# Expert jobs of a fused state-space, MLP and mixture-of-experts kernel: second products three jobs behind, in 256 columns

## The chip, the cores and the metric

The kernel runs on one core of a Trainium2 chip. The metric is the device time of one execution in microseconds (us), as the median of several runs. Profiles come from one further execution each.

## The reference

Three stages, all on 3072 tokens of 256 values. The first is a state-space recurrence over chunks of 32 positions, the second an MLP, the third a mixture of 8 experts of which each token takes one.

```python
# 1: state space, batch 4, 8 heads, 768 positions, head width 32, state 16
M = (Cc @ Bc.T) * L                       # within a chunk, causal decay L
y = M @ xc + (Cc @ state) * exp(cum)      # and from the state before the chunk
state = decay_full * state + sum(Bx)
# 2: MLP, 256 -> 2048 -> 256
x = maximum(x @ w_in, 0) ** 2 @ w_out
# 3: one expert of 8 for each token, 256 -> 1024 -> 256
idx = argmax(xn @ en.T / tau)             # xn, en: rows divided by their norms
gate = softmax(xn @ en.T / tau)[idx]
out[t] = gate[t] * (maximum(x[t] @ w1[idx], 0) @ w2[idx])
```

## The kernel before

The tokens are 24 tiles of 128, in 6 groups of 4 tiles. Every matrix that enters a product is split into two f16 parts, a high and a low one, and a product is the sum of three: high with high, high with low, low with high.

The order of all instructions is written out when the kernel is built, by `weave`. Each piece of work is a generator ("thread") that yields steps: an engine letter (T TensorE, S ScalarE, V VectorE, G GpSimd, Q SyncE's DMA queue), a cost, and the instructions of the step. `weave` keeps a clock for each engine and takes the thread that can start first; among those within a small slack of it, the one with the smallest due time. Due times and some choices of engine are the constants in `DUE`. The order so made is each engine's program: an engine executes its instructions strictly in that order and waits at each for what it needs. `need` and `order` hold a thread back until another has yielded a `mark`.

First come the state-space tiles and, woven with them, the MLP. Its first group runs as f32 products (`unit0`, `unit0_out`), the five others as units (`unit`): a first product of 6 matmuls of 512 columns (L1001), relu and square, a split, and a second product of 12 matmuls of 256 columns (L1037). ScalarE or VectorE squares, by the shares s0 to s2 of `DUE`. Meanwhile the experts' weights are loaded, scaled and split into `W` (`expert`).

When a group of tokens has passed the MLP, `finish` evicts each tile, scales and splits it into a row of f16 halves, turns the row by a DMA transpose on SyncE's queue (`turn`, L387) and makes the logits (L1086). `route` picks each token's expert and its place, and scatters the rows into `xs` in HBM, sorted by expert (L1186). The last 4 values of a row, its "end", hold a factor and the token's number.

A job is a block of 128 rows of one expert. Jobs 0 to 12 (`J1` = 13) are blocks already full from the first five groups. The last group completes the table (`other_jobs`), eight pad blocks are written behind the rows (`pads`, L1518), and the rest follow: 28 jobs always, up to 31 if needed. `job_load` brings a block in, turned, by a DMA transpose (L1333), and its ends by a second, small DMA (L1336), both on SyncE's queue. `job` then has

- a first product into two banks of 512 columns, 12 matmuls (L1363); `job_relu` evicts each bank by ScalarE (high part) and VectorE (low part) into one of 2 buffers `rh`;
- a turn of `rh` into one of 3 buffers `rT` by a DMA transpose on SyncE's queue (L1374);
- a second product of 8 pairs, into a bank of 512 columns: the high part of the rows with both halves of the weights side by side (512 columns, L1390), then the low part with the high half (256 columns, L1392);
- the output: VectorE multiplies the row's factor by the job's (L1398), ScalarE scales columns 256 to 511 (L1400), VectorE scales columns 0 to 255 and adds (L1403), and GpSimd scatters the rows to `out` (L1406).

The expert's number sits in a register of TensorE, so each product's weights have an address that is worked out by a register instruction. The second product of job j is held back until the first product of job j + 2 stands in the order:

```python
yield "order", ("m1j", min(j + 2, JU - 1))
yield "need", ("out", j - 2)
```

At the very start idle TensorE is kept going by dummy products (`keep_warm`, L373).

## Time and profile before

| | |
|---|---|
| median of 3 runs | 530.54 us (529.8 to 534.5) |
| profiled execution | 528.94 us |
| its span, first to last instruction | 527.2 us |
| mean granted TensorE clock | 0.986 of full speed |
| busy: TensorE, VectorE, ScalarE, GpSimd | 95%, 58%, 65%, 30% of the span |
| first product of the first job begins | 358.29 us |
| last instruction of GpSimd ends | 521.1 us |

Times within the execution count from its first instruction. [...] In brackets behind an instruction stands how long its engine was idle before it, and what ended that wait.

### The profile page before, as it was taken

How to read it: one execution, taken by the hardware profiler on the slowest of the kernel's cores; microseconds unless marked ns; L12 is line 12 of the kernel's file. 1: busy time of each engine (PE TensorE's matmuls, PEld its weight loads, DVE VectorE, ACT ScalarE, POOL GpSimd, SP SyncE). 2: the span in 40 equal slices, each digit the busy share in tenths (PEclk: the TensorE clock that was granted, in tenths of full speed). 3: DMA queues.
4: the chain of work that ended last, by engine and by line, in shares of the span. 5: the costliest groups of instructions: out<-in, count | busy, mean ns of one | idle time of the engine just before them, and what ended most of it. 6: DMA issues, size and time to landing. Idle time of an engine off the chain costs nothing. (4 is left out here: it accounts for less than half of the span.)

```text
span 527.2 us, 11441 instructions
## 1 busy us (share of the span) xinstructions
PE 499.4 (95%) x3888; PEld 315.3 (60%) x3888; DVE 308.1 (58%) x856; ACT 342.7 (65%) x725; POOL 159.1 (30%) x189
## 2 busy tenths in 40 slices
PE   7799999999999999999999999999979999998992
PEld 6564456887666676667666766674535555554551
DVE  3668978517988878676457548837345343432330
ACT  6578868119879989999999999865222333322320
POOL 1454657301564337301410320500113311120212
PEclk9999999999999999999999999999979999998998
DMA  8970132424182631293313322025799977887651
GB/s 291 411 272 2 29 92 62 114 108 130 30 205 81 141 101 54 90 203 99 130 72 79 153 90 42 32 52 99 124 143 176 217 158 143 147 134 146 131 118 38
DMA packets 114377, 65.07 MB, mean 123 GB/s; under 512 B 103429, under 2 KB 107791, under 8 KB 111248
## 3 DMA queue, kind: packets, MB, share of 16 engines
q1 hardware_dynamic: 111824, 57.93, 44.9%
q0 software_dynamic: 2496, 6.40, 4.0%
q8 instruction: 34, 0.56, 0.4%
q14 instruction: 23, 0.19, 0.1%
HBM read 32.58 MB, written 8.13 MB: 77 GB/s over the span
## 5 line engine op out<-in xcount | busy, mean ns | idle before, releaser
L1037 PE MATMUL bank<-work 128*128 128x256 f16 x960 | 115.6, 273 | 1.2 <-issue 0.8
L1001 PE MATMUL bank<-work 128*128 128x512 f16 x480 | 114.4, 379 | 0.7 <-ACT work L1006 0.7
L1037 PEld LDWEIGHTS <-work 128*128 128x128 f16 x960 | 92.2, 98 | 20.7 <-issue 1.8
L1390 PE MATMUL bank<-wexp,work 128*128 x224 | 77.7, 392 | 6.7 <-DMA work<-work 6.1
L1363 PE MATMUL bank<-wexp,work 128*128 x336 | 77.6, 381 | 0.4 <-DMA work<-xs 0.4
L1001 PEld LDWEIGHTS <-work 128*128 128x128 f16 x480 | 45.8, 99 | 45.1 <-issue 2.1
L1406 POOL DMA_INDIRECT out<-work x28 | 27.6, 985 | 130.0 <-DVE work L1403 111.3
L1416 ACT ACTIVATE work<-bank 128x512 f16<-128x512 f32 x56 | 32.8, 597 | 46.2 <-PE bank L1363 25.0
L1392 PE MATMUL bank<-wexp,work 128*128 x224 | 62.8, 280 | 0.0
L1418 DVE SCALAR_TENSOR_TENSOR work<-bank,work 128x512 f16<-128x512 f32 x56 | 38.2, 689 | 42.1 <-ACT work L1416 41.8
L1025 POOL TENSOR_TENSOR work<-work 128x512 f16<-128x512 f32 x20 | 24.3, 1217 | 104.5 <-ACT work L1018 90.6
L1363 PEld LDWEIGHTS <-work 128*128 128x128 f16 x336 | 32.9, 99 | 37.8 <-issue 1.4
L706 POOL TENSOR_SCALAR_AFFINE_SELECT wexp<-wexp 128x512 f32<-128x512 f32 x48 | 39.2, 816 | 51.5 <-DVE wexp L698 33.4
L1022 DVE TENSOR_TENSOR work<-work 128x512 f16<-128x512 f32 x60 | 42.6, 713 | 20.0 <-ACT work L1018 18.9
L1006 ACT ACTIVATE work<-bank 128x512 f32<-128x512 f32 x80 | 46.7, 591 | 9.6 <-PE bank L1001 9.3
L1400 ACT ACTIVATE work<-bank,work 128x256 f32<-128x256 f32 x28 | 13.3, 474 | 59.0 <-PE bank L1392 57.1
L1018 ACT CAST work<-work 128x512 f16<-128x512 f32 x80 | 48.8, 613 | 0.8 <-DVE work L1014 0.4
L698 DVE TENSOR_TENSOR wexp<-bank,wexp 128x256 f32<-128x256 f32 x96 | 38.1, 416 | 15.1 <-PE bank L690 9.1
L1390 PEld LDWEIGHTS <-work 128*128 128x128 f16 x224 | 22.4, 100 | 35.4 <-DMA work<-work 7.1
L1403 DVE SCALAR_TENSOR_TENSOR work<-bank,work 128x256 f32<-128x256 f32 x28 | 13.5, 484 | 49.2 <-ACT work L1400 47.2
L1011 ACT ACTIVATE work<-work 128x512 f32<-128x512 f32 x64 | 39.9, 629 | 0.6
L1186 POOL DMA_INDIRECT xs<-work x24 | 28.5, 1190 | 35.9 <-DVE work L1182 14.6
(211 smaller groups left out, 747.9 us busy)
## 6 DMA issues: line engine op xcount, KB each, us to landing
wexp<-in_w SPq DMA_DIRECT2D x8, 1024.0 KB
work<-in_w SPq DMA_DIRECT2D x8, 1024.0 KB
wexp<-in_w_in SPq DMA_DIRECT2D x4, 1024.0 KB
wexp<-in_w_out SPq DMA_DIRECT2D x4, 1024.0 KB
wexp<-in_x SPq DMA_DIRECT2D x6, 512.0 KB
wexp<-in_ct SPq DMA_DIRECT2D x6, 256.0 KB
wexp<-in_bc SPq DMA_DIRECT2D x6, 256.0 KB
xs<-work SPq DMA_DIRECT2D x9, 132.0 KB
```

The source lines that it names most:

```text
L698: V.tensor_tensor(mv, ps.rearrange("p (a b) -> p a b", b=32), eg[:, t, n * q:n * q + n].rearrange("p h q -> p (h q)").unsqueeze(2) .to_bro ...
L706: G.affine_select(out=mm, in_=mm, pattern=[[0, 4], [1, P]], compare_op=ALU.is_ge, fill=0.0, base=0, channel_multiplier=-1)
L1001: T.matmul(p, win[:, wi, kk, f * P:(f + 1) * P], x[:, xi * 2 + kk], start=(n == 0), stop=(n == 5))
L1006: S.activation(r, p, AF.Relu, scale=XK)
L1011: S.activation(r, r, AF.Square)
L1018: S.copy(gh, r)
L1022: V.tensor_tensor(gl, r, gh, ALU.subtract)
L1037: T.matmul(po, gg[:, s], wout[:, wi, f], start=(f == 0 and n == 0 and k % 2 == 0), stop=(f == NF - 1 and n == 2), skip_group_check=True)
L1363: T.matmul(p, xj[i][:, xi * 2 + kk], W[:, bass.ds(e, 1), c0:c0 + 512].rearrange("p a b -> p (a b)"), start=(n == 0), stop=(n == 5))
L1390: T.matmul(po, r[:, f], W[:, bass.ds(e, 1), c0:c0 + 512].rearrange("p a b -> p (a b)"), start=(f == 0), stop=False, skip_group_check=True)
L1392: T.matmul(po[:, 0:DM], r[:, 8 + f], W[:, bass.ds(e, 1), c0:c0 + 256].rearrange("p a b -> p (a b)"), start=False, stop=(f == 7), skip_grou ...
L1418: V.scalar_tensor_tensor(out=rh[:, 1, s], in0=p, scalar=0.0, in1=rh[:, 0, s], op0=ALU.max, op1=ALU.subtract)
```

## The change

1. The second product of job j is held back until the first product of job j + 3; there are 4 buffers `rT` instead of 3, and job j's turn of `rh` waits for the second product of j - 4.
2. The second product runs into 256 columns: 8 times three matmuls of 256 columns, the three parts into the same place. So the output is one ScalarE step that scales by the factor; L1400's buffer and VectorE's addition (L1403) are gone.
3. The ends of a job's rows are loaded by a new thread `job_ends`, issued by ScalarE's queue, after the turn of `rh`; behind it stands VectorE's multiplication of the factors. ScalarE gets registers with the row numbers (`ends_rows`).
4. In the last group `finish` turns the rows by 4 TensorE transposes a tile into bank 3 (f16) and one VectorE copy, instead of the DMA transpose.
5. `pads` waits for the last rows of the first table (`xj`) and no longer for their ends (`fi`).
6. Costs in the threads that `weave` counts with, and all of `DUE`, are others, so the whole order is another.

```diff
-           d0=6.529, m0=251.382, m1=-31.115, u1=21.067, du=31.584, t0=-3.93, t1=-0.257, t2=51.405, t3=-77.002,
...
-           fj=73.378, fe=93.207, oj=-46.052, pd=-14.956, oe=40.303, lj=0, l0=-53.773, v0=0.5, v1=0.75, v2=0.75,
...
+           g0=-87.702, g1=1, g2=0, g3=-57.34, dl=0, dl1=0, s0=558470754, s1=0.25, s2=0.25, bs=2, qx=24.864, qb=8.052,
...
+           emb=83.454, con=43.583, fj=93.688, fe=40.743, oj=85.543, pd=28.762, oe=-59.404, lj=51.301, l0=85.543,
...
+    ident_h = A.take([P], F16)
...
-                free["R"] = s + 3.4
-                th[2] = s + 4.0
+                free["R"] = s + 2.4
+                free["D"] = max(free["D"], s) + 0.5
+                th[2] = s + 3.6
...
-        yield "T", 1.296, (u % 2,)
+        yield "T", 1.307, (u % 2,)
...
-        yield from turn(xo, row[:, 0:2 * DM], 0.45)
+        if g < NGRP - 1:
+            yield from turn(xo, row[:, 0:2 * DM], 0.45)
+        else:
+            for i in (2, 3):
+                yield "need", ("ev", 4 * g + i)
+            yield "order", ("xo", k - 1)
+            pt = bank[3].bitcast(F16)[:, 512 * (k % 2):512 * (k % 2) + 512].rearrange("p (c a) -> p c a", a=P)
+            yield "T", 0.3, (3,)
+            for c in range(4):
+                T.transpose(pt[:, c], row[:, c * P:c * P + P], ident_h)
+            yield "V", 0.35, (3,)
+            V.tensor_copy(xo, pt)
+            yield "mark", ("xo", k)
...
-    rT = [OW.take([16, P], F16) for _ in range(3)]
+    rT = [OW.take([16, P], F16) for _ in range(4)]
     res = [OW.take([DM], F32) for _ in range(6)]
-    tbb = [OW.take([DM], F32) for _ in range(2)]
...
-        yield "Q", 1.27, 0.45
+        yield "Q", 1.33, 0.8, -0.35
         reads_rows(Q.dma_start_transpose(out=xj[i].bitcast(I16), in_=row_at(r, 0, 512)), table)
         yield "mark", ("xj", j)
-        yield "Q", 0.48, 0.06
-        reads_rows(Q.dma_start(fi[i].bitcast(I16), row_at(r, 512, 516)), table)
-        yield "mark", ("fi", j)
...
-        yield "need", ("m2j", j - 3)
-        if j < 3:
+        yield "need", ("m2j", j - 4)
+        if j < 4:
             yield "need", ("m2", NF * NGRP - 1)
-        yield "Q", 2.2, 1.8, 0.8
-        Q.dma_start_transpose(out=rT[j % 3], in_=flat(rh))
+        yield "Q", 2.4, 2.6, -0.5
+        Q.dma_start_transpose(out=rT[j % 4], in_=flat(rh))
         yield "mark", ("rT", j)
+        yield "spawn", job_ends(j, table)
         yield "due", job_due(j)
 
-        yield "order", ("m1j", min(j + 2, JU - 1))
+        yield "order", ("m1j", min(j + 3, JU - 1) if j < JU else j)
...
-        yield "T", 2.6, (pb[j % 2],)
+        r = rT[j % 4]
+        po = bank[pb[j % 2]][:, 0:DM]
+        yield "T", 2.64, (pb[j % 2],)
         for f in range(8):
-            c0 = 4096 + f * 512
-            T.matmul(po, r[:, f], W[:, bass.ds(e, 1), c0:c0 + 512].rearrange("p a b -> p (a b)"), start=(f == 0),
-                     stop=False, skip_group_check=True)
-            T.matmul(po[:, 0:DM], r[:, 8 + f], W[:, bass.ds(e, 1), c0:c0 + 256].rearrange("p a b -> p (a b)"),
-                     start=False, stop=(f == 7), skip_group_check=True)
+            for ri, wi in ((0, 0), (0, 1), (1, 0)):
+                c0 = 4096 + f * 512 + wi * DM
+                T.matmul(po, r[:, 8 * ri + f], W[:, bass.ds(e, 1), c0:c0 + DM].rearrange("p a b -> p (a b)"),
+                         start=(f == 0 and ri + wi == 0), stop=(f == 7 and ri == 1), skip_group_check=True)
...
-        yield "V", 0.1, "L"
-        V.tensor_tensor(ff, fi[i][:, 0:2].bitcast(F32), fjob[:, j:j + 1], ALU.mult)
-        yield "S", 0.47, (pb[j % 2],)
-        S.activation(tbb[j % 2], po[:, DM:2 * DM], AF.Copy, scale=ff)
         yield "need", ("sent", j - 6)
-        yield "V", 0.4, (pb[j % 2],)
-        V.scalar_tensor_tensor(out=res[j % 6], in0=po[:, 0:DM], scalar=ff, in1=tbb[j % 2], op0=ALU.mult, op1=ALU.add)
+        yield "S", 0.36, (pb[j % 2],)
+        S.activation(res[j % 6], po, AF.Copy, scale=ff)
...
+    def job_ends(j, table):
+        i = j % NXJ
+        yield "need", ("rows_s", table)
+        yield "need", ("out", j - 2)
+        yield "need", ("sent", j - NXJ)
+        yield "S", 0.45
+        reads_rows(S.dma_start(fi[i].bitcast(I16), xs[bass.ds(rows_s[j], P), 512:516]), table)
+        yield "V", 0.1, "L"
+        V.tensor_tensor(ffj[j % 2], fi[i][:, 0:2].bitcast(F32), fjob[:, j:j + 1], ALU.mult)
+        yield "mark", ("fi", j)
...
+    def ends_rows(table, ap, n):
+        yield "need", ("tab", table)
+        if table:
+            yield "need", ("jr1", J1 - 3)
+        yield "S", 1.0
+        rows_s.extend(load_regs(ap[0:1, 0:n], n, ACT, DUMMY))
+        yield "mark", ("rows_s", table)
...
-        yield "need", ("fi", J1 - 1)
+        yield "need", ("xj", J1 - 1)
         for e in range(E):
-            yield "Q", 0.86, 0.4
+            yield "Q", 0.6, 0.3
```

## Rows read from the trace of the kernel before

**Rows 1.** Stretches of the whole span: busy time by engine, granted clock, DMA share.

```profile
core 0: us, PE busy (x) PEld busy (x) DVE busy (x) ACT busy (x) POOL busy (x), PEclk, DMA share, GB/s
...
0.00:40.00 40.00, 32.37 (x396) 24.00 (x396) 21.88 (x72) 26.56 (x53) 16.11 (x34) 1.00 0.85 321
...
40.00:358.29 318.29, 314.72 (x2675) 212.20 (x2676) 221.79 (x607) 266.21 (x572) 111.40 (x124) 1.00 0.33 91
...
377.00:396.00 19.00, 14.10 (x89) 7.22 (x87) 8.40 (x36) 4.33 (x9) 2.95 (x3) 0.83 0.85 134
...
250.00:300.00 50.00, 48.93 (x370) 33.70 (x369) 29.31 (x76) 49.66 (x102) 13.28 (x11) 1.00 0.32 114
```

**Rows 2.** Who TensorE waited for, whole span: total us, times, longest.

```profile
PE bank L1390 <- DMA work<-work: 6.1, 3, 2.9
...
PE bank L1086 <- DMA work<-work: 1.3, 3, 0.8
...
PE bank L663 <- DVE work L916: 0.8, 1, 0.8
...
PE bank L1390 <- SPq L1594: 0.6, 1, 0.6
```

**Rows 3.** TensorE in order of time, 378 to 398 us; idle before in brackets.

```profile
378.98 0.38 PE L1390 MATMUL bank<-wexp,work 128*128 x1 [1.08 <-DMA work<-work]
...
390.98 0.59 PE L1390 MATMUL bank<-wexp,work 128*128 x1 [2.94 <-DMA work<-work]
...
397.56 0.38 PE L1390 MATMUL bank<-wexp,work 128*128 x1
```

**Rows 4.** TensorE in order of time, 430 to 484 us.

```profile
430.67 2.75 PE L1363 MATMUL bank<-wexp,work 128*128 x12 [0.41 <-DMA work<-xs]
...
446.24 2.75 PE L1363 MATMUL bank<-wexp,work 128*128 x12
...
448.83 0.38 PE L1390 MATMUL bank<-wexp,work 128*128 x1
...
451.43 1.89 PE L1363 MATMUL bank<-wexp,work 128*128 x8
...
477.01 0.38 PE L1390 MATMUL bank<-wexp,work 128*128 x1 [2.07 <-DMA work<-work]
...
483.91 0.38 PE L1390 MATMUL bank<-wexp,work 128*128 x1
```

**Rows 5.** SyncE's queue in order of time: DMA instructions, start and duration.

```profile
377.80 2.57 SPq L387 DMA_TRANSPOSE work<-work  x2
...
421.71 0.34 SPq L1518 DMA_DIRECT2D xs<-work  x1
...
426.31 2.79 SPq L1333 DMA_TRANSPOSE work<-xs  x2
...
471.36 3.18 SPq L1374 DMA_TRANSPOSE work<-work  x1
```

**Rows 6.** TensorE in order of time, the MLP's last units.

```profile
346.88 1.47 PE L1037 MATMUL bank<-work 128*128 128x256 f16 x12
...
348.19 2.75 PE L1001 MATMUL bank<-work 128*128 128x512 f16 x12
```

**Rows 7.** L1363 (357 to 360 us), L1390 (378.8 to 381): durations, starts.

```profile
L1363 PEldq FUSED_REGOPS  x21: 51/55/65, 357.1 to 359.9; - x21
...
L1363 PE MATMUL bank<-wexp,work x8: 379/379/379, 358.3 to 359.8; 128*128 x8
...
L1390 PEldq FUSED_REGOPS  x8: 55/55/55, 378.9 to 380.8; - x8
```

**Rows 8.** TensorE's groups by line and shape, 40 to 358.2 us.

```profile
L793 PE MATMUL bank<-wexp 128*128 128x128 f32 x40 | 7.8, 278 | 0.0
```

**Rows 9.** Line L1336, whole span: loads of row ends.

```profile
L1336 SPq DMA_DIRECT2D work<-xs x28: 333/430/1082, 351.3 to 479.3; - x28
```

**Rows 10.** VectorE in order of time, the end.

```profile
519.21 0.48 DVE L1403 SCALAR_TENSOR_TENSOR work<-bank,work 128x256 f32<-128x256 f32 x1 [2.84 <-ACT work L1400]
```

## The prediction

> **What bounds the kernel now.** Read the stretches first [rows 1]. Up to 358.29 us TensorE loses 7.63 us of the first 40 (the start, which is also padded with dummy products) and 3.57 us of the next 318: that part is bound by TensorE's own work. The expert jobs follow. [...] Read next who TensorE waited for [rows 2]: the largest entry is L1390, the second product of a job, three times, for the DMA that turns its rows (rT). Last read those places in order of time [rows 3, 4]. In an undisturbed job the first product takes 448.83 - 446.24 = 2.59 us and the second 451.43 - 448.83 = 2.60 us, 5.19 us together [rows 4], and there TensorE is never idle. So a job is bound by columns streamed, and what can be won is the disturbed places, the start, and the tail.

> **What it removes.** Times in us, from the profiled execution.
> The waits of L1390 for rT: 1.08 at 378.98, 2.94 at 390.98 [rows 3], 2.07 at 477.01 [rows 4]; 6.09. Why rT is late: SyncE's queue is served in order. Two of the last group's four row turns (L387) stand in it at 377.80 for 2.57, just where the rT turns are needed, and in the other place one rT turn, issued at 471.36, held the queue for 3.18 by itself [rows 5] and landed some 5.6 after its issue. Three jobs of distance with a fourth rT buffer put one more first and one more second product, 5.2, between a job's first product and its second. Each of the three waits is shorter than that.
> The slower clock behind two of them: from 390.98 to 397.56 a second product and half a first took 6.58 where 2.60 + 1.30 is due, 2.68 lost [rows 3]; from 477.01 to 483.91 a whole pair took 6.90 for 5.19, 1.71 lost [rows 4]. Sum 4.39; with no wait of 2 to 3 us ahead of it the clock has no occasion to fall.
> The logits' wait for the turned rows (L1086), 0.8 at its longest [rows 2]: TensorE now turns them itself. I leave its other two waits standing.
> The wait for job 13's rows, 0.41 [rows 4], and that of the last job for its rT, 0.6 [rows 2], which gets one more product of cover.
> The tail: after the last second product ScalarE scales one half and VectorE adds the other (0.48 [rows 10]); VectorE's step goes. 0.48. On the earlier 27 jobs that step lay beside TensorE's work and its removal is worth nothing.
> Sum removed: 6.09 + 4.39 + 0.8 + 0.41 + 0.6 + 0.48 = 12.77.

> **What it adds.**
> Columns: the second product was 8 x (512 + 256) columns in 16 instructions and is 24 x 256 in 24. The MLP's second product has that very form: 12 of 128x256 take 348.19 - 346.88 = 1.31 [rows 6], so 24 take 2.62 against 2.60. 28 x 0.02 = 0.56.
> Issue: unlike the MLP's, a job's products take their weights' address from a register, and each carries one register instruction on TensorE's sequencer. How fast can that go? Where the sequencer starts ahead of the array it issued 21 of them from 357.1 to 359.9, 2.8 / 20 = 0.14 each; after the wait at 378.9 eight at L1390, with as many of L1392 between, took 1.9, that is 1.9 / 14 = 0.136 each [rows 7]. The array needs 0.109 for 256 columns and 0.216 for 512. So a second product that starts with nothing issued ahead takes 24 x 0.136 = 3.26, 0.64 too long, while a first product gives the sequencer time: 12 x (0.216 - 0.136) = 0.96. Alternating, a job needs 36 x 0.136 = 4.9 of sequencer in 5.21 of array: hidden, with a cover of 0.3. By 359.9 the sequencer was some 13 products ahead of the array (21 issued, 8 begun) [rows 7], and a second product eats about 5 of them. The cover is gone where second products follow each other: the order now ends with four in a row (jobs 24 to 27), and three of them have no first product ahead. 3 x 0.64 less the 0.3 still in hand = 1.6. Bounds: 0 (if the queue holds more) and, where it fails everywhere, a rival below.
> Turning the last group's rows: 16 products of 128 columns. No row has them in f16; half of the 0.109 for 256 columns is 0.055 [rows 6], the f32 turns of L793 cost 7.8 / 40 = 0.195 [rows 8]. Between 0.88 and 3.1 in all; I take 0.88, since a 16-bit product of that width is the nearer form. TensorE pays it in full, as it is the bound. VectorE's four copies of 128x512 (an estimate: at most twice the 0.48 of a 128x256 step [rows 10]) lie beside it.
> [...]
> Row ends on ScalarE's queue: an issue costs 0.43, at most 1.08 [rows 9]. It leaves SyncE, where it stood ahead of rT turns, and lands on ScalarE, which in the jobs is busy for about a quarter of the time (4.33 of 19 [rows 1]): worth nothing either way by itself. But VectorE's multiplication by the ends' factor now stands right behind the issue in VectorE's order, so VectorE waits for the landing, and behind it waits the next job's second relu step. That step has time: the bank it frees is wanted two jobs later, 2 x 5.19 less the first product's 2.59 and the relu steps themselves. Up to some 6 us of landing (an estimate from [rows 4]) it costs nothing.
> Residual: a new order of this length will have some wait of its own; I take one of the removed size, 1.08 + 0.41 = 1.5 (bounds 0 and 4).
> Sum added: 0.56 + 1.6 + 0.88 + 1.5 = 4.54.

> **The first 358 us.** All due times change, so the order of everything does. What it can give back is part of 7.63 + 3.57 idle [rows 1]; it can as well add as much. For it: the embeddings' preparation is put far later, and TensorE waited 0.8 for its VectorE steps [rows 2]; and most squares of groups 2 to 5 move from ScalarE, busy for 49.66 of 50 us where TensorE lost 1.07, to VectorE, busy for 29.31 [rows 1]. I take a gain of 1.0, bounds 5 either way.

> **The sum.** -12.77 + 4.54 - 1.0 = -9.2. The profiled execution took 528.94 (span 527.2 and 1.7 around it), which is 1.6 below the median of the runs, 530.54. So 519.7 by the profiled execution, and 521.3 for the median.

> **Rivals.**
> The gain turns into a wait for job 13's rows. Its row turns were issued at 426.31, after eight pad writes of which the last stood at 421.71 [rows 5], each between rT turns; TensorE already waited for them [rows 4]. If this chain keeps its place in time, all that is saved ahead of 430 is waited for there, and only 2.07 + 1.71 + 0.6 + 0.48 less 0.3 and 1.6 is left: about -3, 527.5. Against it: the chain starts with the last group's logits, which no longer queue for SyncE behind rT turns.
> The new order of the first 358 us loses 5 where I take a gain of 1: 527.3.
> Slower: TensorE's sequencer binds in every job, because it reaches each second product with nothing issued ahead (it stands at a semaphore for rT or for a bank until the array has caught up). Then the 0.64 comes 28 times, 18 us, and the sum is -12.77 + 0.56 + 0.88 + 1.5 - 1.0 + 18 = +7.2: 537.7. It decides when the lead over the array at the start of a second product is below some 5 products. Against it: the 13 products of lead [rows 7].
> A change that doesn't do what it says, with rT still late because the transfers themselves are slow, would keep the 6.09 and the clock's 4.39 in part; the residual's upper bound and the first rival cover it.

> **How the numbers follow.** The forecast has 0.69, job 13's rows 0.13, the lost start 0.10, the starved array 0.08. The forecast's own span, from no residual, no burst and 5 gained at the start to the bounds on the other side (turns at 0.195, residual 4), is 514 to 526. The range takes in the two middling rivals and ends at 529; only the starved array is outside, with a little on the fast side. About 1% is what a measurement here can tell from no change, 525.2 to 535.8: faster 0.72, most of the forecast and the lucky end of the first rival; within 1%, 0.20; slower 0.08.

> **What would show it.** In the profile after: no wait of TensorE at the second product above 1 us, and full clock from 377 to 487 us; the undisturbed job at 5.2 us; register instructions of the second product at 0.136 us, and the last three second products at about 3.2 us instead of 2.6; job 13's first product near 420 us without a wait; L387 at 20 turns, not 24. I am wrong if a job takes 5.3 us or more in the middle of the run, if the first product of job 13 still begins at 430 us, or if TensorE's first job begins more than 5 us from 358.

## The result and the profile after

The changed kernel took 533.88 us (median of 20, 529.6 to 538.9), the kernel before 529.82 (median of 20): 1.010 times as long, 95% interval 1.007 to 1.013. Forecast were 521.3 us and faster, with a range that ends at 529: wrong in size, in sign and in range. By the bounds that the prediction set (525.2 to 535.8) the result is "within 1%", which had 0.20. The profiled execution of those runs fell in a disturbed state (granted clock 0.76 from 20 to 40 us), so all rows of the changed kernel below are of the same kernel run once more (`after_again`: 532.34 us, median of 8; profiled execution 532.66 with a span of 531.0).

Cut both spans at the first job's first matmul and at the end of the last matmul (spans are given to 0.1 us, so a tail is good to 0.05):

| us | before | after | difference | forecast |
|---|---|---|---|---|
| first job begins | 358.29 | 359.44 | +1.15 | -1.0 |
| jobs, first to last matmul | 160.32 | 160.10 | -0.22 | -7.75 |
| tail, last matmul to end | 8.59 | 11.46 | +2.87 | -0.48 |
| span | 527.2 | 531.0 | +3.8 | -9.2 |

Stretches of the changed kernel, columns as in [rows 1]:

```profile
0.00:40.00 40.00, 34.07 (x390) 25.47 (x391) 20.71 (x66) 25.76 (x53) 18.18 (x36) 0.96 0.85 321
40.00:359.44 319.44, 315.59 (x2680) 212.27 (x2679) 247.22 (x661) 246.85 (x525) 103.89 (x117) 1.00 0.33 90
359.44:519.54 160.10, 154.31 (x1060) 100.19 (x1057) 53.28 (x155) 46.37 (x100) 29.28 (x30) 1.00 0.78 143
377.00:396.00 19.00, 18.67 (x139) 12.95 (x138) 11.01 (x46) 5.40 (x12) 6.85 (x7) 1.00 0.92 182
```

The stretch of [rows 1] with the slow clock is mended: from 377 to 396 us TensorE is busy for 18.67 us instead of 14.10, at a granted clock of 1.00 instead of 0.83. The clock is 1.00 through all of the jobs. And yet they last as long as before. In the first 40 us TensorE is idle for 1.7 less than before, from there to the first job for 0.3 more; yet the first job comes 1.15 later, since 2.6 us more of busy time lie ahead of it, some of it at a clock of 0.96 in the first 40 us.

Who TensorE waited for, as in [rows 2]:

```profile
PE bank L1373 <- DVE work L1435: 5.7, 5, 1.8
PE bank L1100 <- DMA work<-work: 2.3, 5, 0.7
```

No wait for rT (the second product is now L1402); the waits of the logits (L1100) all lie ahead of the first job. In its place the first product (L1373) waits for VectorE's relu step (L1435), 5.7 us in five places. TensorE in order of time, first where two of these waits lie, then three later stretches, of which the second has another:

```profile
396.53 2.75 PE L1373 MATMUL bank<-wexp,work 128*128 x12
400.82 1.46 PE L1373 MATMUL bank<-wexp,work 128*128 x6 [1.54 <-DVE work L1435]
404.10 1.46 PE L1373 MATMUL bank<-wexp,work 128*128 x6 [1.83 <-DVE work L1435]
...
419.29 5.94 PE L1402 MATMUL bank<-wexp,work 128*128 x48
425.09 5.34 PE L1373 MATMUL bank<-wexp,work 128*128 x24
430.26 2.78 PE L1402 MATMUL bank<-wexp,work 128*128 x24
433.15 5.34 PE L1373 MATMUL bank<-wexp,work 128*128 x24
...
442.79 2.75 PE L1373 MATMUL bank<-wexp,work 128*128 x12 [1.69 <-DVE work L1435]
...
500.62 18.92 PE L1402 MATMUL bank<-wexp,work 128*128 x144
```

Read the counts; times per product run from start to start, since matmuls overlap (a first one's own duration is 0.379 us, the starts are 2.59 / 12 = 0.216 apart [rows 4, 7]). A job has 12 first and 24 second matmuls. 24 first ones in a row are two jobs; 144 second ones in a row are six. At the start seven first products stand ahead of the first second one (359.44 to 380.59), so first products run up to six jobs ahead, not three: "the first product of job j + 3 stands ahead" is a lower bound in the code, and the order made from the due times goes beyond it. Second products then come in pairs (419.29: 48 matmuls in 5.80 us up to the next start, where 2 x 2.62 are 5.24), and the six that are left over come at the end, in 18.92 us, where six times 2.62 are 15.7.

Why VectorE is late: its relu step waits for ScalarE's (L1433), and that waits until an earlier turn has read the buffer. The row turns (L1384) on SyncE's queue, and who waits for them:

```profile
L1384 SPq DMA_TRANSPOSE work<-work x28: 1669/2194/3616, 363.6 to 506.1; - x28
...
  ACT work L1433: 68.6, 21
...
DMA to landing us min/median/max: 4.3/5.0/7.2
```

There are two buffers `rh`: the relu of job j writes into the one that the turn of job j - 2 reads. One round of a buffer is a turn (5.0) and the relu steps after it (ScalarE's two of 0.6 and the last of VectorE's, 0.68): 6.9 us, and with two buffers one job in some 3.5 us (an estimate from these durations). While first and second products alternate, a first product comes every 5.21 us and the buffers keep up. When first products follow each other it comes every 2.59, and they don't.

The tail, GpSimd in order of time: the scatters of the last jobs' rows to `out` (L1412, and L1406 in the kernel before). In brackets the idle time before each.

```profile
513.52 0.97 POOL L1412 DMA_INDIRECT out<-work  x1 [2.52 <-ACT work L1409]
516.69 0.97 POOL L1412 DMA_INDIRECT out<-work  x1 [2.19 <-ACT work L1409]
519.88 0.97 POOL L1412 DMA_INDIRECT out<-work  x1 [2.21 <-issue]
523.85 0.97 POOL L1412 DMA_INDIRECT out<-work  x1 [3.00 <-issue]
```

Before:

```profile
520.14 0.98 POOL L1406 DMA_INDIRECT out<-work  x1 [1.92 <-DVE work L1403]
```

The last matmul ends at 519.54 and ScalarE's output step at 520.05; the last scatter goes at 523.85. Scatters stand 3.2 to 4.0 us apart, since each writes `out` and so waits until the one before has landed (median 3.2 us from issue). The second of the six rows was ready 2.56 us after the first, whose scatter took 5.0 to land; from there GpSimd is 3.2 to 3.8 behind, and with rows 3.3 to 3.5 apart it doesn't catch up. In the kernel before the last scatter went at 520.14, 1.53 after the last matmul.

### The profile page after: what moved, and what is told of

It is laid out like the page before. It is cut to its first block, busy times and chain, and to the rows that moved or that the text cites. A ratio compares the mean times of both kernels' runs of the same rounds, so it can differ in the third digit from the quotient of the medians.

```text
span 537.1 us, 12108 instructions
## 1 busy us (share of the span) xinstructions
PE 511.1 (95%) x4126; PEld 341.6 (64%) x4126; DVE 322.0 (60%) x881; ACT 319.1 (59%) x678; POOL 153.0 (28%) x185
## 5 line engine op out<-in xcount | busy, mean ns | idle before, releaser
L1039 PEld LDWEIGHTS <-work 128*128 128x128 f16 x960 | 92.3, 98 | 18.7 <-issue 2.0
L1373 PE MATMUL bank<-wexp,work 128*128 x336 | 79.0, 386 | 6.1 <-DVE work L1435 6.1
L1402 PE MATMUL bank<-wexp,work 128*128 x672 | 81.7, 273 | 0.0
L1433 ACT ACTIVATE work<-bank 128x512 f16<-128x512 f32 x56 | 30.6, 594 | 80.1 <-DMA work<-work 66.5
L1402 PEld LDWEIGHTS <-work 128*128 128x128 f16 x672 | 65.8, 98 | 17.1 <-issue 0.9
L1003 PEld LDWEIGHTS <-work 128*128 128x128 f16 x480 | 45.8, 99 | 44.3 <-issue 1.2
L1435 DVE SCALAR_TENSOR_TENSOR work<-bank,work 128x512 f16<-128x512 f32 x56 | 36.3, 686 | 43.4 <-ACT work L1433 41.8
L1373 PEld LDWEIGHTS <-work 128*128 128x128 f16 x336 | 33.0, 99 | 43.2 <-issue 9.6
L1412 POOL DMA_INDIRECT out<-work x28 | 27.3, 976 | 115.1 <-ACT work L1409 77.8
L1027 POOL TENSOR_TENSOR work<-work 128x512 f16<-128x512 f32 x20 | 26.1, 1307 | 100.3 <-ACT work L1020 84.7
L708 POOL TENSOR_SCALAR_AFFINE_SELECT wexp<-wexp 128x512 f32<-128x512 f32 x48 | 35.1, 733 | 58.0 <-DVE wexp L700 48.3
L700 DVE TENSOR_TENSOR wexp<-bank,wexp 128x256 f32<-128x256 f32 x96 | 38.8, 417 | 19.2 <-PE bank L692 12.4
L1024 DVE TENSOR_TENSOR work<-work 128x512 f16<-128x512 f32 x60 | 41.3, 693 | 11.4 <-ACT work L1020 11.1
L1016 DVE SCALAR_TENSOR_TENSOR work<-bank,work 128x512 f32<-128x512 f32 x60 | 40.9, 685 | 10.3 <-ACT work L1008 10.2
L1424 DVE TENSOR_TENSOR work<-work 128x1 f32<-128x1 f32 x28 | 4.5, 160 | 61.7 <-DMA work<-xs 51.1
L1200 POOL DMA_INDIRECT xs<-work x24 | 25.9, 1080 | 43.6 <-issue 33.3
L944 PE MATMUL bank<-work 128*128 128x512 f32 (+1 forms) x80 | 31.4, 527 | 0.0
```

The source lines that it names most:

```text
L700: V.tensor_tensor(mv, ps.rearrange("p (a b) -> p a b", b=32), eg[:, t, n * q:n * q + n].rearrange("p h q -> p (h q)").unsqueeze(2) .to_bro ...
L708: G.affine_select(out=mm, in_=mm, pattern=[[0, 4], [1, P]], compare_op=ALU.is_ge, fill=0.0, base=0, channel_multiplier=-1)
L944: T.matmul(p, wides[0][:, q, 512 * kk + P * i:512 * kk + P * i + P], x32[:, kk, cols], start=(kk == 0), stop=(kk == 1), skip_group_check=True)
L1003: T.matmul(p, win[:, wi, kk, f * P:(f + 1) * P], x[:, xi * 2 + kk], start=(n == 0), stop=(n == 5))
L1016: V.scalar_tensor_tensor(out=r, in0=p, scalar=XK, in1=r, op0=ALU.mult, op1=ALU.mult)
L1024: V.tensor_tensor(gl, r, gh, ALU.subtract)
```

## The experiments

All medians in us; "before" is the median of the kernel before in the same set of runs. Start, jobs and tail are those of the table above, from one profiled execution each. The ratios, with their intervals, are not the quotients of the two medians, which for y2_cap_pads_outs would be 0.993 and for z4_pairs 0.985. y2, y6 and the three z kernels have four runs each, the others eight or ten.

| kernel | median | before | ratio, 95% | start | jobs | tail |
|---|---|---|---|---|---|---|
| after_again | 532.34 | 529.49 | 1.0077 (1.0031 to 1.0124) | 359.44 | 160.10 | 11.46 |
| x1_fixed | 530.05 | 529.49 | 1.0035 (0.9997 to 1.0072) | 361.00 | 156.95 | 13.35 |
| x2_pairs | 532.46 | 529.49 | 1.0071 (1.0024 to 1.0117) | 360.98 | 156.72 | 12.90 |
| x3_noland | 533.24 | 529.04 | 1.0095 (1.0054 to 1.0137) | 358.63 | 160.92 | 11.15 |
| x4_cap | 532.12 | 529.49 | 1.0062 (1.0021 to 1.0104) | 359.64 | 157.30 | 11.26 |
| y1_cap_pads | 526.97 | 527.97 | 0.9967 (0.9931 to 1.0003) | 358.79 | 155.72 | 11.69 |
| y2_cap_pads_outs | 524.28 | 527.97 | 0.9859 (0.9780 to 0.9939) | 360.60 | 154.91 | 8.09 |
| y5_outs | 532.65 | 527.97 | 1.0080 (1.0038 to 1.0121) | 359.44 | 164.21 | 7.85 |
| y6_olddue | 538.03 | 527.97 | 1.0144 (1.0062 to 1.0227) | 364.55 | 159.82 | 11.73 |
| z3_before_pads_outs | 534.88 | 529.04 | 1.0138 (1.0061 to 1.0216) | 358.38 | 165.69 | 8.43 |
| z4_pairs | 521.04 | 529.04 | 0.9876 (0.9814 to 0.9939) | 360.51 | 150.27 | 8.42 |
| z5_regs_later | 522.35 | 529.04 | 0.9881 (0.9822 to 0.9940) | 364.81 | 151.67 | 8.02 |

**The same kernel again.** 

> The changed kernel once more, for a profile at full clock in the start. In the first profile the start ran at 0.83 of the clock and the first job began at 362.5 us. Expected: about 532 us, first job at 358 to 360 us, and the expert jobs still 162 to 163 us from the first matmul to the last, with six second products in a row of 3.2 us each at the end.

The result holds; its profile is the one above. The jobs took 160.1 us and not 162 to 163: at full clock they are shorter than in the first profile (163.2, with a granted clock of 0.83 from 400 to 420 us).

**Is the second product bound by TensorE's sequencer?** The weights' address is made fixed, so that no register instruction is needed. It leaves out the choice of the expert: all second products take expert 0.

```diff
-                T.matmul(po, r[:, 8 * ri + f], W[:, bass.ds(e, 1), c0:c0 + DM].rearrange("p a b -> p (a b)"),
+                T.matmul(po, r[:, 8 * ri + f], W[:, 0, c0:c0 + DM],
```

> The changed kernel, but all second products take the weights of expert 0 at a fixed address, so that the register instruction of each matmul is gone; the order of everything else is the same, and the values are those of expert 0. Theory 'issue' (24 matmuls with a register instruction each take 0.133 us apiece on TensorE's sequencer, more than the array's 0.109): a second product takes 2.62 us wherever it stands, the six at the end 15.7 instead of 19.2, the time falls by 5 to 6 us to about 528. Theory 'turn' (what is lost is first products waiting for relus that wait for the rows' turn by DMA): second products stay at 3.2 us in a row, time within 1 us of the changed kernel.

TensorE and GpSimd in order of time, the end:

```profile
502.07 15.88 PE L1402 MATMUL bank<-wexp,work 128*128 128x256 f16 x144
```

```profile
518.08 0.97 POOL L1412 DMA_INDIRECT out<-work  x1 [2.19 <-issue]
521.27 0.98 POOL L1412 DMA_INDIRECT out<-work  x1 [2.22 <-issue]
524.18 0.98 POOL L1412 DMA_INDIRECT out<-work  x1 [1.93 <-issue]
```

The same 144 matmuls take 15.88 instead of 18.92 us, 0.110 each instead of 0.131, and the pairs of second products fall to 5.24: the cost is the sequencer's. The jobs get 3.15 shorter. But the tail grows by 1.9, as the scatters are the bound at the end: counted from the first job, the last one goes at 163.18 instead of 164.41 us. Some 1.2 of the 3.15 reach the end by the profiles, 2.3 by the medians, where 5 to 6 had been expected; so the issue cost is real, and removing it alone makes this order no faster than the kernel before.

**The second product in pairs again**, 8 x (512 + 256) columns in 16 matmuls, with VectorE's output step, in the new order.

```diff
+            T.matmul(po, r[:, f], W[:, bass.ds(e, 1), c0:c0 + 512].rearrange("p a b -> p (a b)"), start=(f == 0),
...
+            T.matmul(po[:, 0:DM], r[:, 8 + f], W[:, bass.ds(e, 1), c0:c0 + 256].rearrange("p a b -> p (a b)"),
...
+        S.activation(tbb[0], po[:, DM:2 * DM], AF.Copy, scale=ff)
+        V.scalar_tensor_tensor(out=res[j % 6], in0=po[:, 0:DM], scalar=ff, in1=tbb[0], op0=ALU.mult, op1=ALU.add)
```

> The changed kernel in its own order, but the second product again as 8 pairs of 512 and 256 columns, with the output by ScalarE and VectorE. Theory 'issue': 16 register instructions instead of 24, 2.60 us for each second product also in a row, 5 us faster than the changed kernel less 0.5 for VectorE's step at the end, about 529. Theory 'turn': no change of more than 1 us.

Who TensorE waited for:

```profile
PE bank L1374 <- DVE work L1438: 6.6, 6, 1.9
```

The second products go at 2.60 in a row too, as expected. The jobs get 3.38 shorter and the tail 1.4 longer; counted from the first job, the last scatter goes 1.85 earlier, but the median does not move, where 3 us were expected. It agrees with the last run. The waits for VectorE's relu (L1438 here) stay, 6.6 in six places, where the changed kernel has 5.7 in five. So the form of the second product alone isn't what makes the order slow.

**Does VectorE, standing behind the landing of the ends, hold the relu steps up?** The factor is taken from a value that is ready, so that VectorE doesn't wait for the ends (the outputs' factors are then others).

```diff
-        V.tensor_tensor(ffj[j % 2], fi[i][:, 0:2].bitcast(F32), fjob[:, j:j + 1], ALU.mult)
+        V.tensor_tensor(ffj[j % 2], fjob[:, j:j + 1], fjob[:, j:j + 1], ALU.mult)
```

> The changed kernel in its own order, but VectorE's factor of a job is made from a value that is ready, so that VectorE no longer waits for the row ends to land (51 us of waits in all); the factors are wrong, everything else is done. Theory 'landing' (VectorE stands behind the landing and its relu steps come late, so first products wait): the waits of first products fall from 5.7 us to below 2, and the time to 529 or less. Rival 'turn' (VectorE's relu waits for ScalarE's, and that for the turned rows of two jobs before): the waits stay, time within 1 us of the changed kernel.

Who TensorE waited for:

```profile
PE bank L1373 <- DVE work L1435: 5.4, 5, 1.8
```

5.4 instead of 5.7, the longest as long, and no gain. VectorE's 49.9 us of waits for the ends (which land 2.7 us after their issue in the median) are idle time that nobody pays. This theory falls; the prediction had costed it at nothing.

**The order as the prediction had it**: a first product may not stand ahead of the second product of four jobs before.

```diff
             yield "order", ("m1j", j - 1)
+            yield "order", ("m2j", j - 4)
             yield "T", 1.307, (hb[j % 2][q],)
```

> The changed kernel, but a first product may stand in the order only behind the second product of four jobs earlier, so that first and second products alternate at a distance of exactly three jobs; in the changed kernel first products stand up to six jobs ahead, with 2 buffers for relu and 4 for turned rows. Theory 'turn': the five waits of first products for VectorE's relu (6.1 us) and the slow clock behind them go, 6 to 8 us faster, about 526. Theory 'issue' alone: the pairs of second products in the middle and half of the row of six at the end go, 3.5 us faster, about 530. Both: about 524.

Who TensorE waited for, and SyncE's queue in order of time:

```profile
PE bank L1374 <- DMA work<-xs: 6.6, 1, 6.6
```

```profile
390.45 0.37 SPq L1545 DMA_DIRECT2D xs<-work  x1
391.25 3.00 SPq L1385 DMA_TRANSPOSE work<-work  x1
395.36 0.35 SPq L1545 DMA_DIRECT2D xs<-work  x1
...
416.83 1.67 SPq L1385 DMA_TRANSPOSE work<-work  x1
419.71 0.34 SPq L1545 DMA_DIRECT2D xs<-work  x1
421.06 1.82 SPq L1385 DMA_TRANSPOSE work<-work  x1
426.23 7.78 SPq L1346 DMA_TRANSPOSE work<-xs  x6
```

Every wait for the relu is gone, so they came from the run-ahead. What is left, but for 0.34 at 406.5, is one wait of 6.61 ahead of 428.91, for job 13's rows: the rival that had 0.13. Eight pad writes stand one by one between row turns, 390.45 to 419.71, and most of these turns wait in the queue for their job's relu steps; the loads come after them, at 426.23, where they stood at 426.31 before [rows 5]. In this order the chain kept its place in time, as that rival says. The 524 to 530 that had been expected did not come. The profile lies 2.2 us below the median of its ten runs, so what the cap alone brings is not settled beyond "no measurable gain".

**Cap, and the pads in one step** instead of eight:

```diff
+        yield "Q", 4.8, 2.4
         for e in range(E):
-            yield "Q", 0.6, 0.3
```

> The version with the capped lead, and all eight pad blocks issued in one go on SyncE's queue instead of one between each two turns of rows. Theory 'job 13': the capped version lost what it had won in one wait of 6.6 us for job 13's rows, and behind it at the slow clock, because the eight pads stood 30 us long between turns in SyncE's order. Then that wait goes, the jobs take about 150 us from first to last matmul, and the time is 521 to 524 us. Rival 'slow turns': the DMA queue itself is full, job 13's rows come no earlier than 426 us, and the time stays at 530 or more.

SyncE's queue, then TensorE and its sequencer:

```profile
390.50 7.50 SPq L1545 DMA_DIRECT2D xs<-work  x8
398.09 10.67 SPq L1385 DMA_TRANSPOSE work<-work  x3
409.17 3.83 SPq L1346 DMA_TRANSPOSE work<-xs  x3
```

```profile
409.48 1.01 PE L1374 MATMUL bank<-wexp,work 128*128 x2 [3.33 <-issue]
```

```profile
L1292 PEldq TENSOR_LOAD <-work x2: 1306/2282/3259, 356.2 to 406.0; - x2
```

The pads are through by 398 and the loads begin at 409: job 13 no longer waits. A third wait comes up in its place: TensorE's sequencer loads the second table's expert numbers into its registers, which took 3.26 us from 406.0, and for that time issues nothing (no weight load starts between 405.89 and 409.49). In the kernel before the same load took 3.05 from 413.9 and cost 0.1: there 15 matmuls had been issued ahead, here none. The clock falls in that wait (0.83 in 400 to 420; the weight loads of the first product behind it start 0.43 us apart, where its matmuls need 0.216). So the time stays 3 us above the 521 to 524 expected.

**And the scatters to `out` made independent** of each other (they write different rows):

```diff
+        made = G.indirect_dma_start(out=out, out_offset=bass.IndirectOffsetOnAxis(ap=fi[i][:, 2:4].bitcast(I32), axis=0),
...
+        no_wait(made, outs, "other rows")
+        outs.append(made.ins)
```

> As the version with capped lead and pads in one go, and besides the scatters to the output, which write different rows, no longer wait for one another. Theory 'tail': in the changed kernel 11.4 us pass from the last matmul to the end, 8.6 before, because GpSimd's scatters each wait for the landing of the one ahead (3.2 to 4.0 us apiece) and fall behind a row of second products. Then the tail is 8.5 us and the time 2 to 3 us below the version without it, about 519 to 521. Rival: GpSimd itself takes that long for a scatter, and nothing changes.

TensorE and GpSimd, the end:

```profile
504.26 11.25 PE L1404 MATMUL bank<-wexp,work 128*128 x96
```

```profile
510.44 0.97 POOL L1414 DMA_INDIRECT out<-work  x1 [1.65 <-SPq L1625]
513.07 0.98 POOL L1414 DMA_INDIRECT out<-work  x1 [1.65 <-SPq L1625]
516.29 0.97 POOL L1414 DMA_INDIRECT out<-work  x1 [2.25 <-ACTq L1625]
```

Four second products at the end, as the prediction had counted them, 0.77 above 4 x 2.62. The scatters go 2.6 to 3.2 us apart, as their rows are made; the last one 0.78 behind the last matmul. The tail is 8.09 for 11.69, and the scatters' wait for landing is shown to be what made it long. The median falls by the 2 to 3 us expected. Faster than the kernel before, by 1.4% by the ratio and 0.7% by the medians.

**Only the independent scatters, without cap and with eight pad steps.**

> The changed kernel with that one edit alone: scatters to the output do not wait for one another. Theory 'tail': 2.5 to 3 us faster than the changed kernel, about 529.5 us, with the expert jobs otherwise as they were (160 us from first to last matmul, waits of first products for VectorE's relu). Rival: no change.

The tail falls to 7.85 as it should, and the jobs take 164.21: the waits for the relu are 8.0 here, in six places. They move between 4.7 and 8.0 in the kernels that keep the run-ahead; why they are longest here wasn't settled. No gain, where 2.5 to 3 us had been expected. The pads in one step without the cap were not run.

**The old due times with the new code.**

```diff
-DUE = dict(jm=51.927, r0=79.033, r1=93.021, r2=12.918, r3=60.968, sv=0.395, ss=0.078, sg=0.283, ct0=90.237, cm=255,
...
+DUE = dict(jm=12.44, r0=90.613, r1=170.672, r2=-53.19, r3=48.138, sv=0.353, ss=0.126, sg=0.415, ct0=97.079, cm=255,
...
```

> All parts of the change, but with the due times of before: the first products then stand exactly three jobs ahead, and the order of the first 358 us is near that of before. Theory 'due times' (the parts are sound and the new order spends the gain): the waits of first products for VectorE's relu are gone, the first job begins at 358 us, and the time is 521 to 526 us, the upper end if job 13's rows are waited for. Rival 'parts' (row ends on ScalarE's queue with VectorE waiting for them, and second products of 24 matmuls, cost what the rest saves): 530 us or more.

TensorE in order of time:

```profile
364.55 1.67 PE L1373 MATMUL bank<-wexp,work 128*128 x7
...
435.56 1.86 PE L1373 MATMUL bank<-wexp,work 128*128 x4 [7.26 <-DMA work<-xs]
```

Products alternate throughout, with one wait for a relu, of 0.40: the run-ahead is made by the due times, not by the code. Among them `jm` is the time by which a job's thread is due ahead of its second product, 12.4 us before and 51.9 in the change, ten jobs instead of two; it was not changed alone. Job 13's rows are late by 7.26 again. And the first job begins 5.1 later than with the new due times: this code needs them for the first 358 us. The time is one that the rival (530 or more) allows, but not by its cause: of some 11.7 us that these jobs lose, 9.4 lie at job 13's wait and in the slow clock behind it (0.83 from 420 to 440 us).

**Control: the pads in one step and independent scatters in the kernel before.**

> The kernel before, with the two edits that are not part of the change: all pads in one go, and scatters to the output that do not wait for one another. A control: does the gain of the last version (5 us under the kernel before) come from these two alone? Theory 'parts and order': before they bind nothing (0.4 us of wait for job 13's rows, a tail of 8.6 us), so the time stays within 1.5 us of the kernel before, 528 to 530. Rival: it falls to 524 too, and the change itself gives nothing.

Who TensorE waited for:

```profile
PE bank L1391 <- issue: 6.0, 1, 6.0
PE bank L1391 <- DMA work<-work: 5.3, 5, 2.2
```

Slower by 1.4%, where neither side had expected it. The tail stays (8.43 for 8.59: there the scatters were no bound, since second products came one by one to nearly the end). In the order that comes out here the register load (2.90 us from 410.7) falls where nothing covers it, in a wait of 6.05 that ends at 413.80, and rT is late in five places; what held the sequencer from 407.75 to 410.7 was not settled. So the two edits by themselves don't make the kernel before faster; what they are worth there without that wait is not shown.

**The last version with the second product in pairs again** (z4_pairs: y2_cap_pads_outs with the edit of x2_pairs), **and with the register load two jobs later** (z5_regs_later):

```diff
-        yield "need", ("m1j", J1 - 4)
+        yield "need", ("m1j", J1 - 2)
```

> As the version with capped lead, pads in one go and independent scatters, but the second product as 8 pairs of 512 and 256 columns, with the output by ScalarE and VectorE. Theory 'issue': where first and second products alternate, the 24 register instructions are hidden behind the first product, so only the row of four at the end (0.8 us) and 28 times 0.02 us come off, and 0.5 us of VectorE's step is added: within 1 us, 523 to 525. Rival: 24 instructions cost in every job, and pairs are 3 us or more faster.

> As the version with capped lead, pads in one go and independent scatters, but TensorE's registers with the second table's experts are loaded two jobs later, after the first product of job 11 instead of job 9. In that version TensorE idled 3.3 us at 408 us, while its sequencer spent 3.3 us on that load with nothing issued ahead, and ran at the slow clock behind it. Theory: with products issued ahead the load is hidden, as in the kernel before, and 3 to 5 us go: 520 us. Rival: the load stalls the array wherever it stands, and the time stays at 524.

Who TensorE waited for in z4_pairs, in the jobs, and its register loads:

```profile
PE bank L1376 <- DVE work L1431: 1.3, 1, 1.3
...
PE bank L1404 <- DMA work<-work: 0.5, 1, 0.5
PE bank L1163 <- DVE work L1414: 0.4, 1, 0.4
```

```profile
L1293 PEldq TENSOR_LOAD <-work x2: 1312/1464/1617, 357.9 to 407.6; - x2
```

The pairs give the shortest median, 521.04 us. Of the 4.64 that its jobs are shorter than those of y2_cap_pads_outs, the end's burst accounts for 0.69 (10.56 us for 11.25) and the columns for about 0.5; most of the rest lies at the register load, where y2 lost 5.75 (3.34 of wait, with a slow second product ahead of it, 0.92, and a slow first one behind it, 1.49) and this one 1.5, and 0.6 more in a wait for rT just ahead. (The wait of 1.3 is named after L1431, which the first product does not read; it ends at 409.40, and the load at 409.20.) Here the load itself was also shorter, 1.62 for 3.27, so how much of that is the pairs and how much the load's luck is not told apart. With fewer register instructions per job (28 for 36) the sequencer has more lead: a second product's first one goes 3.5 us ahead of its matmul here while products alternate, 2.6 to 2.7 in y2 (and 3.52 in the kernel before, from 489.10 on). The median is 3.2 us below that of y2, as the rival had it, but in another set of runs. In z5 the wait moved with the load: the load took 1.92 from 422.4, the wait 1.51; its profiled execution began its first job at 364.81 with the clock at 0.71 in 20 to 40 us, so its span is no measure, its median of 522.35 is. By the ratios both beat the kernel before by 1.2%, y2 by 1.4%; the intervals don't tell these three apart.

## Why the prediction was wrong

It went wrong in the sum added and in the tail; what it removed was removed.

**Removed: right.** The rT waits, the last group's logits' wait, job 13's 0.41 and the slow clock are gone in this profile. Worked out from the rows: the jobs' due time (28 x 5.19 and 1.4 of the last group's logits) is 146.7, and before they took 160.32, so 13.6 was lost; forecast for the jobs were 12.3.

**"Three jobs of distance": the step that failed.** It was read as the order, and is a lower bound. Residual 1.5 (bounds 0 and 4) was to hold the new order's waits; measured 5.66 for the relu, and 0.6 more of slower groups around it. Shown by x4_cap and y6_olddue, where the run-ahead goes and these waits go with it, but for 0.40 in y6_olddue.

**The issue burst: right in mechanism, mis-sized.** The register instructions of the six second products at the end, all of them and then from 509 us on:

```profile
L1402 PEldq FUSED_REGOPS  x144: 55/55/55, 499.0 to 519.2; - x144
...
L1402 PEldq FUSED_REGOPS  x73: 55/55/55, 509.0 to 519.2; - x73
```

One goes every 20.2 / 143 = 0.141 us, where 0.136 was read off [rows 7]. (18.92 / 144 = 0.131 is less since the first matmuls had been issued ahead.) The sequencer keeps up while products alternate (2.62 for a second product, as forecast), and the rival with a starved array in every job is refuted. Two sizes were wrong. The prediction counted four second products in a row; there are six, and six pairs besides (5.52, 5.87, 5.80, 5.67, 5.33 and 5.24 us). Measured against 2.62 each: 3.2 at the end, 2.0 in the pairs, 0.5 in two single ones, 5.7 in all for 1.6. x1_fixed and x2_pairs show it. And the cover was not 0.3 us: the first of these instructions goes at 499.0 for a matmul that starts at 500.62, 1.6 ahead, so the first two products lose next to nothing. In y2_cap_pads_outs, with the four as counted, the cover was 2.6, and the four cost 0.77, half of the 1.6.

**The tail: the sign was wrong.** -0.48 for VectorE's step, with the last scatters taken to follow the last product as before. The prediction had not asked what six or four results in a row do to GpSimd, where each scatter waits for the last one's landing. +2.87; shown by y2 and y5, where the wait goes and the tail is 8.1 and 7.85.

**The turns by TensorE: right.** Four of them (L1090) take 0.22 us from their first start to the next first product's:

```profile
363.33 0.39 PE L1090 MATMUL bank<-work 128*128 128x128 f16 x4
363.55 1.46 PE L1373 MATMUL bank<-wexp,work 128*128 x6
```

That is 0.055 each, the value taken; 0.88 in all. A single turn's own duration is 0.216 to 0.219, but they follow each other at a quarter of that. The granted clock is 1.00 from 360 to 380 us, where all 16 lie.

**The first 358 us:** -1.0 forecast, +1.15 measured, inside the bounds of 5. In the nine profiles with the new due times in which the granted clock was at least 0.9 in the first 20 us and 1.00 in the next, the first job began between 358.6 and 361.0. A slower clock in the first 20 us does not explain a late first job: the four at 1.00 there began at 360.5 to 361.0, the five at 0.91 at 358.6 to 359.6. What does is open.

**Job 13's rows: the rival was right for the capped order only.** In the changed kernel the loads began earlier than before, and job 13's first product, at 425.09, did not wait:

```profile
420.63 2.91 SPq L1346 DMA_TRANSPOSE work<-xs  x2
```

With the cap they stand at 426.23, and the rival is there with 6.6 us. Of the prediction's three signs of being wrong only the job time came (160.1 / 28 = 5.7 us); relu waits and scatters were not among the signs.

Sum check: from -9.2, add 4.8 for the relu waits and the groups around them, 4.1 for the issue, 3.35 for the tail, 2.15 for the start, less 1.3 for what was removed beyond the forecast: +3.9; measured +3.8.

## What to carry to other kernels

Before costing a change of order, write out the order that the program really has: a rule "not before" says nothing on how far ahead a step runs, and the two buffers that kept up here while products alternated (a first product every 5.21 us) failed when first products came in bunches (every 2.59). For each burst ask the next engines down the line: here matmuls in a row outran the sequencer, and their results outran the scatters, so that saving in one was given back in the other. When one wait on a path is removed, cost the next two in line at once; here rT, the relu, job 13's rows, the register load and the scatters stood one behind the other, and only versions that met the relu, job 13's rows and the scatters were clearly faster.

## What the runs showed of the hardware

Second products with register addresses went at 0.137 to 0.145 us per matmul once the sequencer had lost its lead (the third to sixth of the six at the end, in the changed kernel's first profile: 0.138, 0.137, 0.145 and 0.141), where their 256 columns take 0.109 while products alternate. In that profile and in the one of the kernel before the lead never exceeded 18 matmuls; before, it stood at 18 at 244 of the jobs' 784 register instructions. No burst there had more cover.

A long wait did not always bring the clock down: in y5_outs TensorE was idle for 3.64 us up to 402.90, and the granted clock stayed at 1.00 from 350 to 440 us. In the kernel before it fell to 0.50 at 389.65, within a wait of 2.94, and at 478.39, 1.4 us behind a wait of 2.07. That it would not fall without a wait of 2 to 3 us was the prediction's estimate from these two places; what brings it down no run shows.

Scatters that may overlap went 2.60 us apart at the end of z4_pairs, as fast as their rows were made; serialised by their landing they go 3.2 to 4.0 apart in the changed kernel.
